# A transformer block in fp32: the MLP on four tiles at a time, attention items of eight heads, and the residual in DRAM

## The chip, the core and the metric

The kernel runs on one core of a Trainium2 chip. Its engines are TensorE (PE, with weight loads as PEld), VectorE (DVE), ScalarE (ACT), GpSimd (POOL) and SyncE (SP, which issues every DMA here). The metric is device time in microseconds; smaller is better. The kernel before takes 536.42 us, the median of 3 runs from 535.81 to 536.80.

## The reference

One sequence of S=2048 tokens with D=512. The block is pre-norm attention followed by a pre-norm MLP, each with a residual. Attention has 32 heads of 16; a token looks at itself and at seven earlier tokens, two apart (W=8, dilation 2). The MLP has F=1792 hidden columns and a squared ReLU.

```python
def _A_ref(x, wqkv, wo):
    qkv = (x @ wqkv).reshape(B, S, 3, H, Dh)   # q, k, v by head
    idx = pos[:, None] - off[None, :]          # off = arange(8) * 2
    logits = jnp.einsum("bhsd,bhswd->bhsw", q, kg) * scale
    logits = jnp.where(mask[None, None, :, :], logits, -1e9)
    attn = _softmax(logits, axis=-1)
    o = jnp.einsum("bhsw,bhswd->bhsd", attn, vg)
    return o.reshape(B, S, D) @ wo

def _B_ref(x, w1, b1, w2, b2):
    h = jnp.einsum("bsd,df->bsf", x, w1) + b1
    r = jnp.where(h > zero, h, zero)
    return jnp.einsum("bsf,fd->bsd", r * r, w2) + b2

h = x + _A_ref(_layernorm(x), A_wqkv, A_wo)
h2 = h + _B_ref(_layernorm(h), B_w1, B_b1, B_w2, B_b2)
```

## The kernel before

**Precision.** Every operand of a product is split into a high part, rounded to fp32r by ACT (`hi`, L115), and the rest, subtracted by DVE or POOL (`lo`, L118). A product is three sums of four matmuls over K: high by high, low by high, high by low (`mm3`, L172 to L177). Each matmul's shape in the profile is the number of columns that it streams.

**Tiles.** The 2048 tokens are 16 tiles of 128. The even and odd tokens of each half form a chain, so that the dilated window is contiguous rows of a chain; a chain of a half is four tiles. An index s from 0 to 7 stands for a pair of tiles (RI=2).

**The qkv stage.** For each tile and each of four column groups, 12 matmuls of 384 columns; ACT evacuates (`evac`, L412), and SP stores q, k and v into a DRAM scratch `qkv_d` (`store`). The first four tiles run group by group while the weights are prepared, then pairs of tiles (`first_phase`). Meanwhile `weight_job` loads and splits wo and w1.

**Attention.** An item is a pair s and a group pair of 8 heads, 32 items in all. Its windows of k and v come from `qkv_d`, as two halves j of four heads each, in two buffers a half. For s=0 and s=1 one load of 11 rows serves both. DVE multiplies q and k (`dots`, L272), sums over the head (L306, L320), adds the mask in the first half, subtracts the maximum (L333, L335); ACT exponentiates (L339); DVE sums, inverts and scales (L302, L309, L315) and multiplies with v (`weigh`, L283); POOL adds the eight window rows in a tree of three additions (L292), whose last one writes `o`. The halves j go one after the other. `attention()` is a generator: it yields the planned DVE time of what it has just written, and an item's second half is interleaved with the first half of the next item.

**Order.** The program is written slot by slot. `at` and `after` set chores for a slot; `end_slot` adds the slot's planned PE time, runs the chores, and lets `pump` take attention steps while the planned DVE time (times SLOW=1.1) is behind the planned PE time. `o_T(s, j)` first pumps until the items of s are written, then transposes o on PE; `wo_product` multiplies by wo into a `tr` bank; `h_add` (DVE, L475) adds the residual and takes statistics; `h_norm` (ACT, POOL) normalises and adds b2 to the residual, which stays in SBUF; `h_T` transposes the normalised tile.

**The MLP.** For each pair s, 14 hidden blocks f: `mlp1` is 12 matmuls of 256 columns (both tiles) into one of two `mm` banks; `hidden` is ReLU, square and cast on ACT (L509, L510, L115) and the low part on POOL, or on DVE for the last pair (HV=7); `mlp2` of block f-3 (LAG=3) is three matmuls of 512 columns for each tile into its accumulator bank, `acc0` or `acc1`. In the slots of pair s the o transposes of s+1 come at f=3 and 4 and its wo products at f=6 and 7. `finish` (DVE, L537) adds the residual, and SP writes the output. w2 is loaded and split during s=0 into the memory that wqkv had.

PSUM has eight banks: two `tr`, two `mm`, `acc0`, `acc1`, one for q (`qp`) and one for the exponentials (`ex`). SBUF rows of 2 KB are shared by many names under one tag with 15 buffers (ROWS).

## Time and profile before

| | us |
|---|---|
| median of 3 runs | 536.42 |
| the profiled execution, its own time | 534.84 |
| its span, first to last instruction | 533.1 |
| PE busy | 520.7 |
| PEld busy | 479.1 |
| DVE busy | 376.1 |
| POOL busy | 317.9 |
| ACT busy | 262.1 |

The granted clock was 1.00 over the whole span. A row of a group gives the line, engine, operation, tiles (out<-in), shapes and count; after the first bar the busy time and the mean duration in ns; after the second the idle time of that engine just before those instructions and what ended it. A row of a timeline begins with the start and the duration in us; a row with x4 is four in succession, and its duration is that of the four together, with the drain of the last. Matmuls overlap, so their cost is read from start to start. A row of windows gives the stretch, its length, the busy time and count of PE, PEld, DVE, ACT and POOL, the clock, the share of the DMA engines and GB/s. A row of DMA issues gives the count, the size of one and the median time from issue to landing.

### The profile page before, as it was taken

To read this page: it belongs to the slowest core of one execution; us is meant where nothing else is said; L and a number is where in the kernel's file an instruction comes from. 1 tells how busy PE (TensorE), PEld (TensorE's weight loads), DVE (VectorE), ACT (ScalarE), POOL (GpSimd) and SP (SyncE) were. 2 spreads that over 40 slices of the span, in tenths; PEclk is the share of its full clock that TensorE was granted. 3 is DMA by queue.
4 is the path that set the end of the run, shared out by engine and by line. 5 is a ranking of instruction groups with operands and counts; after the bars stand their busy time and mean duration, and the time that the engine had idled before them with its cause. 6 is when DMAs were issued, how large, how long until landed. Compare 5 with 4: busy or idle time off the path is not lost.

```text
span 533.1 us, 9022 instructions
## 1 busy us (share of the span) xinstructions
PE 520.7 (98%) x3186; PEld 479.1 (90%) x3186; DVE 376.1 (71%) x569; ACT 262.1 (49%) x607; POOL 317.9 (60%) x435
## 2 busy tenths in 40 slices
PE   6999999999999989999999999999999999999996
PEld 5899999999999868988989898898989889898995
DVE  5569999887897898996998699599869502202111
ACT  4524554455248446545636454563645445254541
POOL 4515499687495398778678677867867852251000
PEclk9999999999999999999999999999999999999999
DMA  8577979687587453633643364364434102001001
GB/s 251 155 233 196 298 234 317 201 269 239 159 252 263 135 157 91 191 116 102 182 142 108 111 190 119 100 183 137 112 106 140 44 0 81 1 0 41 2 0 41
DMA packets 70661, 75.96 MB, mean 143 GB/s; under 512 B 6744, under 2 KB 47704, under 8 KB 70616
## 3 DMA queue, kind: packets, MB, share of 16 engines
q1 hardware_dynamic: 70616, 75.39, 46.7%
q8 instruction: 25, 0.41, 0.3%
q14 instruction: 20, 0.16, 0.1%
HBM read 58.50 MB, written 16.91 MB: 141 GB/s over the span
## 4 chain that ended last, share of the span: by engine, by line
PE 61%; POOL 2%; DVE 0%; ACT 0%; issue 0%; POOLq 0%
PE mm L177 27%; PE acc L530 9%; PE acc L532 9%; PE acc L531 9%; PE wo L177 6%; PE tr L155 2%; POOL pr L292 1%; POOL rl L118 1%; POOL h L483 0%; POOL rs L134 0%; DVE pr L283 0%; POOL rs L132 0%; DVE h L537 0%; ACT hh L115 0%; POOL o L292 0%
## 5 line engine op out<-in xcount | busy, mean ns | idle before, releaser
L292 POOL TENSOR_TENSOR pr<-pr 128x512 f32<-128x512 f32 (+1 forms) x128 | 133.0, 1039 | 47.6 <-DVE pr L283 42.5
L118 POOL TENSOR_TENSOR rl<-r,rh 128x256 fp32r<-128x256 f32 x98 | 72.1, 739 | 82.9 <-ACT rh L115 73.6
L509 ACT ACTIVATE r<-mm,b_sb 128x256 f32<-128x256 f32 x112 | 53.3, 476 | 123.1 <-PE mm L177 112.3
L272 DVE TENSOR_TENSOR pr<-qp,k 128x1024 f32<-128x1024 f32 x64 | 76.0, 1187 | 5.8 <-ACT qp L216 3.5
L283 DVE TENSOR_TENSOR pr<-ex,v 128x1024 f32<-128x1024 f32 x64 | 77.9, 1217 | 2.8
L532 PE MATMUL acc<-w_h,rl 128*128 128x512 f32 x192 | 75.0, 391 | 2.7 <-POOL rl L118 2.7
L530 PE MATMUL acc<-w_h,rh 128*128 128x512 f32 x192 | 76.5, 398 | 0.0
L531 PE MATMUL acc<-w_l,rh 128*128 128x512 f32 x192 | 75.9, 395 | 0.0
L177 PE MATMUL mm<-hh,w_h 128*128 128x256 f32 x448 | 72.5, 284 | 0.0
L177 PEld LDWEIGHTS mm<-hh,w_h 128*128 128x128 f32 x448 | 66.4, 189 | 6.5
L177 PE MATMUL mm<-hl,w_h 128*128 128x256 f32 x448 | 72.0, 283 | 0.0
L177 PE MATMUL mm<-hh,w_l 128*128 128x256 f32 x448 | 72.0, 283 | 0.0
L177 PEld LDWEIGHTS mm<-hl,w_h 128*128 128x128 f32 x448 | 61.8, 192 | 0.0
L177 PEld LDWEIGHTS mm<-hh,w_l 128*128 128x128 f32 x448 | 61.7, 192 | 0.0
L412 ACT COPY y<-mm 128x384 f32<-128x384 f32 x64 | 30.1, 480 | 63.6 <-PE mm L177 40.0
L177 PE MATMUL mm<-wq_h,xh 128*128 128x384 f32 x256 | 56.7, 342 | 0.3 <-ACT wq_h L115 0.3
L177 PE MATMUL mm<-wq_l,xh 128*128 128x384 f32 x256 | 55.3, 335 | 0.2 <-DVE wq_l L118 0.2
L177 PE MATMUL mm<-wq_h,xl 128*128 128x384 f32 x256 | 55.0, 335 | 0.4 <-DVE xl L118 0.4
L118 DVE TENSOR_TENSOR hl<-tr,hh 128x256 fp32r<-128x256 f32 x32 | 12.1, 418 | 56.8 <-ACT hh L115 56.8
L510 ACT ACTIVATE r<-r 128x256 f32<-128x256 f32 x112 | 46.9, 418 | 3.5
L115 ACT CAST rh<-r 128x256 fp32r<-128x256 f32 x112 | 45.6, 407 | 3.6
L532 PEld LDWEIGHTS acc<-w_h,rl 128*128 128x128 f32 x192 | 36.1, 188 | 11.8 <-POOL rl L118 3.6
(78 smaller groups left out, 869.3 us busy)
## 6 DMA issues: line engine op xcount, KB each, us to landing
k<-qkv_d SPq DMA_DIRECT2D x48, 288.0 KB, 2.8
v<-qkv_d SPq DMA_DIRECT2D x48, 288.0 KB, 2.7
qkv_d<-y SPq DMA_DIRECT2D x32, 384.0 KB, 3.9
xt<-in_A_x_dram SPq DMA_DIRECT2D x16, 256.0 KB, 4.2
q<-qkv_d SPq DMA_DIRECT2D x32, 128.0 KB, 2.8
h<-in_A_x_dram SPq DMA_DIRECT2D x16, 256.0 KB, 4.0
out_dram<-h SPq DMA_DIRECT2D x16, 256.0 KB, 3.2
raw<-in_B_w_dram SPq DMA_DIRECT2D x16, 224.0 KB, 4.3
```

What stands on the lines that cost most here:

```text
L115: nc.scalar.copy(dst, src)
L118: eng.tensor_tensor(out=dst, in0=src, in1=h, op=ALU.subtract)
L177: nc.tensor.matmul(ps, l(k), r(k), start=(n == 0), stop=(n == 3 * KB - 1))
L272: nc.vector.tensor_tensor(out=pr.rearrange("p i w h d -> p i w (h d)"), in0=qp[:, j].unsqueeze(2).to_broadcast([P, RI, W, GC]), in1=kwin, ...
L283: nc.vector.tensor_tensor(out=p2, in1=vwin, op=ALU.mult, in0=e1[:, :, :, j * GH:(j + 1) * GH].unsqueeze(4).to_broadcast([P, RI, W, GH, DH]))
L292: nc.gpsimd.tensor_tensor(out=dst, in0=p2[:, :, :w], in1=p2[:, :, w:2 * w], op=ALU.add)
L412: nc.scalar.copy(y[:, :, t % RI * GC:(t % RI + 1) * GC], ps[:, :3 * GP].rearrange("p (j c) -> p j c", j=6))
L509: nc.scalar.activation(r, ps, AF.Relu, bias=b1_sb[:, f:f + 1])
L510: nc.scalar.activation(r, r, AF.Square)
L530: nc.tensor.matmul(a, rh[:, js], w2_h[f], start=(f == 0), stop=False)
L531: nc.tensor.matmul(a, rh[:, js], w2_l[f], start=False, stop=False)
L532: nc.tensor.matmul(a, rl[:, js], w2_h[f], start=False, stop=(f == FB - 1))
```

## The change

Three things change together, and the constants of the plan with them.

*Attention.* G becomes 4: a group has eight heads and 128 columns, and an item is done with one `dots`, one sum and one `weigh` of 2048 elements a partition. k and v have one buffer each of nine rows, loaded for every s, also for s=1. q, ex and the maximum share one PSUM bank (`att`).

*MLP.* The pairs are put in GROUPS of (2, 2, 2, 1, 1): three groups of four tiles and two of two. A wide group streams 512 columns in `mlp1`; its units are single products, first mlp1(f), then mlp2(f-2), alternately (LAG=2). It uses `acc0` to `acc3`, two `mm` banks and one `tr` bank. The transposed activations lie in `actT_h` and `actT_l`, one buffer that the qkv stage uses too. The hidden block's ReLU is written back to PSUM. While a wide group runs, the o transposes of the next group's tiles come at units 12, 15, 18 and 21 and their wo products two units later. `g < HV` (4) puts the low part on POOL for all but the last group.

*Residual.* `h_norm` stores h plus b2 into a DRAM scratch `h_d`; it is loaded again before `finish` (`load_out`): the first two tiles' near the end of the group, the last two of a wide group's after the accumulation, between the finishes. ROWS becomes 7.

```diff
-G = 8
+G = 4
-ROWS = 15
-LAG = 3
-SLOW = 1.1
+ROWS = 7
+LAG = 2
+SLOW = 1.05
-HV = 7
-WJ = 2
+GROUPS = (2, 2, 2, 1, 1)
+HV = 4
...
+    h_d = dram.tile([NS, RI, P, D], F32, name="h_d")
+    actT_h = wpool.tile([P, R, KB, P], F32R, name="actT_h")
+    actT_l = wpool.tile([P, R, KB, P], F32R, name="actT_l")
+    sq = wpool.tile([P, R * P], F32, name="sq")
...
+    att_ps = psum.tile([P, D], F32, name="att")
...
+        def dots(n):
+            pr = att.tile([P, RI, W, GH, DH], F32, name="pr")
+            nc.vector.tensor_tensor(
+                out=pr.rearrange("p i w h d -> p i w (h d)"),
+                in0=qp.unsqueeze(2).to_broadcast([P, RI, W, GC]),
+                in1=window(ks[n], [1, GC]), op=ALU.mult)
+            load_k(n + 1)
+            return pr
...
+        hn[s, j] = row("hn")
+        norm_apply((s, j), hn[s, j], h, nc.scalar)
         nc.gpsimd.tensor_tensor(out=h, in0=h, in1=b2_sb, op=ALU.add)
+        nc.sync.dma_start(h_d[s, j], h)
...
+        nc.scalar.activation(ps, ps, AF.Relu, bias=b1_sb[:, f:f + 1])
+        nc.scalar.activation(r, ps, AF.Square)
+        hi(rh, r)
...
+    def mlp1(g, n, f):
+        ps = psum.tile([P, n * P], F32, name="mm", tag="mm", bufs=2)
+        fs = slice(f * P, (f + 1) * P)
+        mm3(ps, lambda k: w1_h[:, k, fs], lambda k: w1_l[:, k, fs],
+            lambda k: actT_h[:, :n, k, :], lambda k: actT_l[:, :n, k, :])
+        at(1, hidden, g, n, f, ps)
+
+    def mlp2(f, acc, js):
+
+        rh, rl = hid[f]
+        for l, r, last in ((rh, w2_h, False), (rh, w2_l, False), (rl, w2_h, True)):
+            for j in js:
+                nc.tensor.matmul(acc[j], l[:, j * P:(j + 1) * P], r[f],
+                                 start=(f == 0 and l is rh and r is w2_h),
+                                 stop=(f == FB - 1 and last))
...
+    O_T, WO, H_T = (34, 36, 38, 40), (36, 38, 40, 42), (44, 45)
...
+    for n, t in enumerate(groups[0]):
+        if n >= 2:
+            h_T(t, n)
+    run(due)
...
+        if wide:
+            steps = [12 + 3 * n for n in range(len(nxt))]
...
+        for j, t in enumerate(tiles):
+            if j >= 2:
+                at(0, load_out, t)
+            at(0, finish, t, acc[j])
```

## The prediction

> **What bounds the kernel now.** First the page: busy shares, then the chain of work that ended last.

> ```profile
> span 533.1 us, 9022 instructions
> PE 520.7 (98%) x3186; PEld 479.1 (90%) x3186; DVE 376.1 (71%) x569; ACT 262.1 (49%) x607; POOL 317.9 (60%) x435
> PE 61%; POOL 2%; DVE 0%; ACT 0%; issue 0%; POOLq 0%
> ```

> PE is the bound, and what counts is its spacing from start to start, not its busy time. The chain in order of time merges twelve matmuls into a row:

> ```profile
> 407.03 1.43 PE mm L177 x12
> 409.85 2.72 PE wo L177 x12
> ```

> Twelve of 256 columns take 1.43 us, 119 ns each; twelve of 512 columns take 2.72, 227 ns each. PE's timeline gives the other forms, and PE's waits:

> ```profile
> 183.81 0.64 PE L177 MATMUL mm<-hh,w_h 128*128 128x256 f32 x4
> ...
> 185.25 0.40 PE L530 MATMUL acc<-w_h,rh 128*128 128x512 f32 x1
> ...
> 186.63 0.64 PE L177 MATMUL mm<-hh,w_h 128*128 128x256 f32 x4
> ...
> 192.27 0.50 PE L532 MATMUL acc<-w_h,rl 128*128 128x512 f32 x1 [0.75 <-POOL rl L118]
> ...
> 200.17 0.50 PE L532 MATMUL acc<-w_h,rl 128*128 128x512 f32 x1 [1.99 <-POOL rl L118]
> ...
> 126.55 0.85 PE L177 MATMUL mm<-wq_h,xl 128*128 128x384 f32 x4
> 127.24 0.86 PE L177 MATMUL mm<-wq_l,xh 128*128 128x384 f32 x4
> 127.94 0.60 PE L155 MATMUL tr<-ident,o 128*128 128x128 f32 x4
> 128.29 0.95 PE L177 MATMUL mm<-wq_h,xh 128*128 128x384 f32 x4
> ```

> The second product (L530 to L532) has six matmuls from 185.25 to 186.63, 230 ns each; a slot of both products has 2.82 (183.81 to 186.63); the 384-column ones take 0.69/4 = 173 ns, four transposes 0.35 us. So a matmul costs about 13 ns beyond 0.417 ns a column, whatever its width. After the start, PE waits only at the two marked rows, 2.7 us.

> Next I asked how late the attention is, since every o transpose on PE needs it. Windows, DVE's timeline and POOL's, and PE's:

> ```profile
> 46.70:240.00 193.30, 190.50 (x1150) 180.29 (x1149) 174.86 (x260) 99.48 (x226) 138.93 (x185) 1.00 0.68 208
> 45.45 1.21 DVE L283 TENSOR_TENSOR pr<-ex,v 128x1024 f32<-128x1024 f32 x1
> 236.49 1.23 DVE L283 TENSOR_TENSOR pr<-ex,v 128x1024 f32<-128x1024 f32 x1
> 237.63 1.21 DVE L320 TENSOR_REDUCE lg<-pr 128x64 f32<-128x1024 f32 x1
> 238.76 1.22 DVE L283 TENSOR_TENSOR pr<-ex,v 128x1024 f32<-128x1024 f32 x1
> 244.72 0.47 POOL L292 TENSOR_TENSOR o<-pr 128x128 f32<-128x128 f32 x1
> 260.33 0.60 PE L155 MATMUL tr<-ident,o 128*128 128x128 f32 x4
> ```

> The first item's last weighing ends at 46.7, the sixteenth's (last of s=3) at 240.0, its sum on POOL at 245.2, and PE fetches s=3 at 260.3: 15 us of margin. Fourth figure of the window: DVE is busy 174.9 of 193.3 us, idle 18.4.

> **The change, part by part.** *First product.* 1008 matmuls of 256 columns become 504 of 512: 2x119.2 - 226.7 = 11.7 ns each, **-5.9 us**. Bounds: -5.9, or 0 if a moving operand in four pieces of 128 (actT) costs the 13 ns back; the nearest row, wo, has whole rows; I take -5.9. [...] The rows above have 13 ns at all three widths, and the measurement decides.

> *Second product.* In the wide groups 504 of its matmuls run four tiles in a row on one w2 slice, at 230 ns before. Bounds 0 and -1.5 us (504 x 3 ns, down to wo's 227); I take **-0.7**.

> *The two POOL waits* go: mlp2(f) now stands four units (11 us) behind mlp1(f), where it stood three slots of 2.82 us. What is late next is not rl but o, below. **-2.7** (bounds -2.7 and 0).

> *Attention instructions.* Rows by line and shape:

> ```profile
> L283 DVE TENSOR_TENSOR pr<-ex,v 128x1024 f32<-128x1024 f32 x64 | 77.9, 1217 | 2.8
> L315 DVE TENSOR_TENSOR ex<-ex,sm 128x128 f32<-128x128 f32 x32 | 9.1, 283 | 0.0
> L335 DVE TENSOR_TENSOR lg<-lg,mx 128x128 f32<-128x128 f32 x32 | 19.3, 602 | 1.1
> L333 DVE TENSOR_REDUCE mx<-lg 128x16 f32<-128x128 f32 x32 | 12.5, 390 | 0.0
> L302 DVE TENSOR_REDUCE sm<-ex 128x16 f32<-128x128 f32 x32 | 8.9, 279 | 8.1 <-ACT ex L339 8.1
> L292 POOL TENSOR_TENSOR pr<-pr 128x512 f32<-128x512 f32 x64 | 84.7, 1323 | 42.6 <-DVE pr L283 42.5
> L292 POOL TENSOR_TENSOR pr<-pr 128x256 f32<-128x256 f32 x64 | 48.3, 755 | 5.0
> L118 POOL TENSOR_TENSOR rl<-r,rh 128x256 fp32r<-128x256 f32 x98 | 72.1, 739 | 82.9 <-ACT rh L115 73.6 <-issue 9.2
> ```

> L283 against L315 is 1.04 ns an element, so 2048 elements take 2.28 us where two of 1024 took 2.43 (2.2 from start to start, where one of 1024 has 1.14: 236.49, 237.63, 238.76). Three such pairs save 0.45 us an item, and mx in PSUM brings L335 nearer to L315, 0.32: some 0.8 us an item, 12 over fifteen items. A POOL chain of three adds takes 2.46 + 1.32 + 0.76 = 4.5 us. None of this is on PE's path by itself; it is worth what it brings o forward.

> *The deadline moves.* Group 0 holds four tiles, and s=3 is fetched within it. From the first o transposes (127.94, 53 of 64 qkv done, 14 of 16 tiles transposed) PE has eleven qkv of 12x173 ns = 22.9, six wo = 16.3, 18 units of 12x228 ns = 49.3 and twelve sets of transposes = 4.3 to do: 220.7, with the entry wait below **221.7**, against 260.3. DVE: 46.7 + 174.9 - 12 = 209.6 if it never idles, 228 if it idles as before; with POOL's 4.5 us o is ready between 214.1 and 232.5. Two orders tie it to PE's time T at that place. DVE's ol of (2,1) follows that tile's transposes at T-11.3, and after ACT's copy DVE does 0.6 + 2.2 + 0.75 + 2.2 us: weighing done at T-4.5. POOL does rl of f=9 first: that product ends one second product and one wo before T, at T-5.5, ACT's three operations take 1.9, rl 1.3, so the adds start at T-2.2 and o is ready at T+2.3 or later. Bounds +0 (PE never waits) and +10.8 (232.5); I take **+2.4**, by the tied rows. Where ACT's 1.9 is from: 256 columns have 1.30, and 512 some 0.21 more each (oh 584 against hh 375 ns):

> ```profile
> L509 ACT ACTIVATE r<-mm,b_sb 128x256 f32<-128x256 f32 x112 | 53.3, 476 | 123.1 <-PE mm L177 112.3 <-POOL rl L118 9.5
> L510 ACT ACTIVATE r<-r 128x256 f32<-128x256 f32 x112 | 46.9, 418 | 3.5
> L115 ACT CAST rh<-r 128x256 fp32r<-128x256 f32 x112 | 45.6, 407 | 3.6
> L115 ACT CAST hh<-tr 128x256 fp32r<-128x256 f32 x32 | 10.3, 375 | 22.0 <-PE tr L155 22.0
> L115 ACT CAST oh<-tr 128x512 fp32r<-128x512 f32 x16 | 9.3, 584 | 5.6 <-PE tr L155 4.1 <-DVE w_l L118 1.5
> ```

> *Group entry.* The last two h_T stand directly ahead of the first wide product, so PE waits for ACT's copies: 0.27 for a transpose to end and 2x0.58 us, less the second's transposes, 0.35: **+1.0** (0, if ACT lies ahead, to +2, if an evacuation stands before them).

> *The residual in DRAM.* At a wide boundary SP's order is out 0, out 1, load hf 2, out 2, load hf 3, out 3; each out waits for DVE, and DVE's finish of tile 2 and 3 for the load. Issues and landings:

> ```profile
> 211.07 0.89 SPq L539 DMA_DIRECT2D out_dram<-h  x2
> out_dram<-h SPq DMA_DIRECT2D x16, 256.0 KB, 3.2
> h<-in_A_x_dram SPq DMA_DIRECT2D x16, 256.0 KB, 4.0
> k<-qkv_d SPq DMA_DIRECT2D x48, 288.0 KB, 2.8
> L537 DVE TENSOR_TENSOR h<-acc,h 128x512 f32<-128x512 f32 x16 | 10.5, 683 | 4.3 <-PE acc L532 4.2
> ```

> Finishes 0 and 1 end about 1.4 us after the boundary; then twice (issues 0.6 + landing L + finish 0.68): with L of 2.8, 4.0 and 3.2 between them, tile 3 is finished at 9.6, 12.0 or 10.4. PE wants acc3 after three units and three matmuls, 8.9. Two boundaries matter (before the narrow groups acc2 and acc3 are not accumulators): 2 x 0.7 to 2 x 3.1; I take **+2.4**. Queued behind on SP: k of the next item but one; behind finish on DVE: the whole attention, 8 to 9 us. In group 1 h_add(4,0) must free the only tr bank for the next o transposes. DVE has fourteen long instructions of 2.2, four shares of 0.73 (L302, a reciprocal and L315, start to start), five shifts of 0.64 (L333 and L335 without its wait), ol and h_add ahead, 38 us, and ends at 10.4 + 38 = 48.4; PE is there after 15 units, one wo and one set of transposes, 44.1. With PE's own 1.2 lost that is 3.1 short if DVE's sum is exact; bounds 0 and 5; I take **+1.5**. In group 2 the next o is asked for later and the loss is hidden.

> *Hidden.* k and v single-buffered: a k load starts when dots ends and has logits, shares, weighing and shift (6 us) to land; 576 KB at 2.8 us for 288 lands in some 4 to 5. Reloading k and v for s=1 adds some 4 MB before 126 us, where DMA is at its fullest:

> ```profile
> 80.00:100.00 20.00, 20.00 (x122) 19.93 (x121) 18.33 (x28) 9.86 (x21) 17.28 (x23) 1.00 0.93 288
> ```

> There the cover is thin; what it costs is DVE idle, part of the 0 to 10.8 above. ACT's three wide operations (some 1.9 us) fit in 5.5; the h_d writes wait for POOL and share SP with k and v.

> *Sum.* -5.9 - 0.7 - 2.7 + 2.4 + 1.0 + 2.4 + 1.5 = **-2.0 us**, of which -9.3 is gain. The profiled execution took 534.84 us (span 533.1), so 532.8 there; the median of the runs shown is 536.42, 1.6 above it, so **534.4**.

> **The rivals.** *A. Attention falls behind (slower).* DVE idles in the first half as before (18.4 us), so o of s=3 comes at 232.5 and PE stands 10.8 us rather than 2.4; the same idle share (9.5%) over group 1's 38 us adds 3.6. 534.4 + 8.4 + 3.6 = **546.4**. It decides once DVE idles over 10 us between 47 and 217 (209.6 + 10 + 4.5 = T+2.4). For it: the deadline comes forward by 39 us while DVE gains 12, and DMA at 0.93. Against: part of the 18.4 was DVE waiting for PE, which costs nothing when DVE is late.

> *B. All waits hide (faster).* DVE is early at every finish and every o, and the hf loads land in under 2.8 us. Only gains: 536.4 - 9.3 = **527.1**; with the second product's bound 526.3 (another 0.8). For it: item idle in the early rows is small. Against: POOL's in-order place behind rl.

> *C. The wide product is not cheaper.* Four pieces per moving operand cost the 11.7 ns back: **540.3**. For it: no row shows that operand. Against: 13 ns is the same at 256, 384 and 512. [...]

> **How the numbers follow.** Forecast 0.42, A 0.27, B 0.24, C 0.07. The measurement tells 0.2% (1.1 us) from nothing. The forecast's own range, 531 to 538, is centred 2.0 below before: 0.28 faster, 0.08 the same, 0.06 slower. B adds 0.24 to faster; A and C 0.34, of which 0.02 falls in the middle (A in part) and 0.32 is slower. Faster 0.52, same 0.10, slower 0.38. The range reaches from just under B's lower end, 526, into A, 546.

> **What would show it.** Wide mm rows at twelve to 2.72 us (C wrong); finish rows of the wide boundaries with DVE idle behind hf's DMA twice, and a PE gap before acc of tile 3 near 1 us; a PE gap at the o transposes of s=3 of 1 to 5 us (A: about 11, B: none); no PE wait for rl. Wrong altogether if PE stands in the qkv stage, where I count nothing, or if k's landing stops DVE on every item.

## The result, and the profile after

The changed kernel takes **590.56 us**, the median of 4 runs (588.18 to 591.21), where the kernel before, on the same chip, takes 536.12. The ratio is 1.1009, 95% interval 1.0973 to 1.1045: 54 us slower. The prediction, 534.4 with a range of 526 to 546, was wrong. The page of the profiled execution (its own time 588.18), cut to span, busy shares, PE's clock by slices, and the chain that ended last:

```profile
span 586.4 us, 7471 instructions
PE 533.6 (91%) x2682; PEld 463.5 (79%) x2682; DVE 379.0 (65%) x457; ACT 230.1 (39%) x465; POOL 291.5 (50%) x297
PEclk9999999999899997979999989988897999999999
PE 39%; DVE 31%; DMA 10%; POOL 9%; issue 4%; ACT 3%; SPq 2%; DVEq 0%; POOLq 0%; ACTq 0%
```

Before, PE had 61% of the chain and no other engine over 2%; now DVE, DMA and POOL have half of it. The account can be made from these rows and those of before. PE stood 586.4 - 533.6 = 52.8 us, before 533.1 - 520.7 = 12.4: **40.4 us of new stalls**. PE's busy time rose by 12.9 us, and 40.4 + 12.9 = 53.3 is the difference of the spans. The busy time rose although the work became cheaper: with the clock at 1.00 throughout, the same 2682 PE instructions take 516.2 us (pool_light, below), 4.5 less than before. So some 17 us have to be explained, and most of them are stretches in which the clock was granted at half: the trace has seven, 41 us in all, in which PE was busy 29.6 us, twice what that work needs at full clock (twelve matmuls 5.27 us against 2.72, below). That is **some 15 us**; the other 2 to 3 are not accounted for. Where PE stood, from the windows up to the first wide product and on from there:

```profile
46.00:178.90 132.90, 123.93 (x705) 118.21 (x704) 111.39 (x138) 55.12 (x120) 86.10 (x96) 0.99 0.73 243
180.00:586.40 406.40, 367.72 (x1752) 305.67 (x1752) 236.90 (x277) 153.63 (x302) 190.19 (x170) 0.95 0.34 111
```

and from its waits (us in total, times, longest):

```profile
PE wo L187 <- DVE ol L123: 14.3, 4, 5.3
PE tr L171 <- DVE actT_l L123: 10.2, 3, 6.4
PE tr L171 <- POOL o L302: 5.3, 1, 5.3
PE acc L539 <- DVE hf L550: 4.1, 2, 3.4
```

Nine microseconds in the qkv stage (132.90 - 123.93), where before it never stood, and 39 behind it, where before it stood some 7; the longest waits are for DVE. PE's timeline shows both what was right and what a stall costs:

```profile
207.06 1.07 PE L539 MATMUL acc<-w_h,rh 128*128 128x512 f32 x4
...
209.78 1.07 PE L187 MATMUL mm<-actT_h,w_h 128*128 128x512 f32 x4
...
212.50 1.07 PE L539 MATMUL acc<-w_h,rh 128*128 128x512 f32 x4
...
226.66 2.07 PE L187 MATMUL wo<-wo_h,oh 128*128 128x512 f32 x4 [5.34 <-DVE ol L123]
...
231.93 1.08 PE L187 MATMUL mm<-actT_h,w_h 128*128 128x512 f32 x4
```

Twelve wide matmuls take 2.72 us (209.78 to 212.50), as predicted. The twelve of wo behind a stall of 5.34 take 5.27 (226.66 to 231.93). The windows (the clock is the third figure from the end) say why:

```profile
218.00:225.00 7.00, 3.31 (x15) 2.42 (x13) 6.93 (x6) 3.40 (x7) 5.72 (x4) 1.00 0.26 85
225.10:231.90 6.80, 5.24 (x12) 4.13 (x13) 6.64 (x9) 0.66 (x2) 1.18 (x1) 0.50 0.45 148
231.90:246.00 14.10, 14.10 (x65) 11.47 (x63) 13.73 (x17) 5.61 (x10) 8.07 (x8) 1.00 0.43 134
```

The stall begins at 221.3; some 3.7 us into it the clock goes to 0.50, and it stays there for 6.8 us. Another 6.8 us of half clock begin in each of the stalls near 247, 332, 389 and 444 us, and 3.4 us in the one at 147 us and behind the one at 417 us.

**POOL's chain.** Groups of POOL's adds and of DVE's mask add, the same add (L325) before, and POOL and DVE on the timeline of after:

```profile
L302 POOL TENSOR_TENSOR pr<-pr 128x1024 f32<-128x1024 f32 x32 | 77.7, 2428 | 79.4 <-DVE pr L295 79.4
L302 POOL TENSOR_TENSOR pr<-pr 128x512 f32<-128x512 f32 x32 | 41.2, 1288 | 2.5
L302 POOL TENSOR_TENSOR o<-pr 128x256 f32<-128x256 f32 x32 | 24.2, 756 | 2.5
...
L270 DVE TENSOR_TENSOR lg<-lg,mask 128x128 f32<-128x128 f32 x16 | 15.9, 996 | 0.0
```

```profile
L325 DVE TENSOR_TENSOR lg<-lg,mask 128x128 f32<-128x128 f32 x16 | 6.6, 412 | 0.2
```

```profile
206.20 4.13 POOL L302 TENSOR_TENSOR pr<-pr 128x1024 f32<-128x1024 f32 x2 [4.37 <-DVE pr L295]
206.64 2.48 DVE L270 TENSOR_TENSOR lg<-lg,mask 128x128 f32<-128x128 f32 x1
```

An item's adds are now one stretch of 2.43 + 1.29 + 0.76 = 4.5 us, and what the program has behind it on POOL came after it in the trace; before, a half's three adds were 2.5. DVE's mask add, of the same size as before, takes 2.48 us in these rows, as long as POOL's first add beside it (2.43 on average). What else stands behind the adds on POOL: the weight splits of the qkv stage. SP's and ACT's waits between 46 and 180 us, of after and of before:

```profile
SPq L460 <- POOL w_l L123: 20.4, 4, 5.4
SPq L460 <- POOL rs L137: 7.3, 2, 5.8
ACT y L419 <- DMA qkv_d<-y: 49.5, 16, 6.5
```

```profile
SPq L450 <- POOL w_l L118: 3.5, 1, 3.5
ACT y L412 <- DMA qkv_d<-y: 10.4, 5, 3.6
```

The weight loads (L460) took rows of a ring of 15 before; now they share the five buffers of rl and rh, which POOL frees late. (The smaller number of buffers is not the reason by itself: pool_only below has the same five, and SP's 20.4 us are 5.8 there.) SP's queue stands behind them, the stores stand behind SP, and ACT waits for a free y. The three small POOL operations that give the second norm its factors (`rs`) stand behind the adds too. ACT's waits for them over the whole span, of after and of before:

```profile
ACT hn L155 <- POOL rs L141: 45.9, 10, 8.0
```

```profile
ACT hn L150 <- POOL rs L136: 6.8, 3, 3.9
```

Lastly the boundary at 290 us, SP, DVE and PE:

```profile
290.52 0.32 SPq L211 DMA_DIRECT2D v<-qkv_d  x1
291.12 0.94 SPq L552 DMA_DIRECT2D out_dram<-hf  x2
292.15 0.44 SPq L545 DMA_DIRECT2D hf<-h_d  x1
298.00 0.33 SPq L552 DMA_DIRECT2D out_dram<-hf  x1
298.43 0.37 SPq L545 DMA_DIRECT2D hf<-h_d  x1
...
297.28 0.69 DVE L550 TENSOR_TENSOR hf<-acc,hf 128x512 f32<-128x512 f32 x1 [5.58 <-DMA hf<-h_d]
301.24 0.69 DVE L550 TENSOR_TENSOR hf<-acc,hf 128x512 f32<-128x512 f32 x1 [3.27 <-DMA hf<-h_d]
...
301.98 0.50 PE L539 MATMUL acc<-w_h,rh 128*128 128x512 f32 x1 [3.42 <-DVE hf L550]
```

The order is the predicted one, load, finish, out, load, finish; the first load, issued behind a load of v, lands 5.0 us after its issue, and DVE waits 8.9 us in two pieces with one finish between them.

### The profile page after: what moved, and what is told of

It is laid out like the page before. It is cut to its first block, busy times and chain, and to the rows that moved or that the text cites. A ratio compares the mean times of both kernels' runs of the same rounds, so it can differ in the third digit from the quotient of the medians.

```text
span 586.4 us, 7471 instructions
## 1 busy us (share of the span) xinstructions
PE 533.6 (91%) x2682; PEld 463.5 (79%) x2682; DVE 379.0 (65%) x457; ACT 230.1 (39%) x465; POOL 291.5 (50%) x297
## 4 chain that ended last, share of the span: by engine, by line
PE 39%; DVE 31%; DMA 10%; POOL 9%; issue 4%; ACT 3%; SPq 2%; DVEq 0%; POOLq 0%; ACTq 0%
PE mm L187 16%; PE acc L539 15%; DVE pr L295 8%; PE wo L187 7%; DVE pr L254 6%; DVE lg L263 5%; POOL pr L302 5%; DMA xt<-in_A_x_dram 4%; DMA hf<-h_d 2%; DVE lg L270 2%; PE tr L171 2%; DMA h<-in_A_x_dram 1%; DVE actT_l L123 1%; DVE w_l L123 1%; DVE st L131 1%
## 5 line engine op out<-in xcount | busy, mean ns | idle before, releaser
L302 POOL TENSOR_TENSOR pr<-pr 128x1024 f32<-128x1024 f32 x64 | 118.9, 1858 | 81.9 <-DVE pr L295 79.4
L123 POOL TENSOR_TENSOR rl<-sq,rh 128x512 fp32r<-128x512 f32 (+1 forms) x56 | 64.4, 1151 | 115.4 <-ACT rh L120 61.6
L295 DVE TENSOR_TENSOR pr<-att,v 128x2048 f32<-128x2048 f32 x32 | 73.3, 2291 | 4.6 <-DMA v<-qkv_d 1.9
L254 DVE TENSOR_TENSOR pr<-att,k 128x2048 f32<-128x2048 f32 x32 | 73.0, 2280 | 4.7 <-ACT att L248 3.6
L263 DVE TENSOR_REDUCE lg<-pr 128x128 f32<-128x2048 f32 x32 | 73.0, 2280 | 0.6
L187 PE MATMUL mm<-actT_h,w_h 128*128 128x512 f32 (+1 forms) x280 | 65.6, 357 | 1.2 <-ACT actT_h L120 1.2
L187 PE MATMUL mm<-actT_l,w_h 128*128 128x512 f32 (+1 forms) x280 | 63.1, 347 | 1.9 <-DVE actT_l L123 1.9
L187 PE MATMUL mm<-actT_h,w_l 128*128 128x512 f32 (+1 forms) x280 | 64.1, 351 | 0.0
L187 PE MATMUL mm<-wq_h,actT_h 128*128 128x384 f32 x256 | 58.2, 349 | 1.6 <-ACT actT_h L120 1.1
L539 PE MATMUL acc<-w_h,rh 128*128 128x512 f32 x192 | 54.9, 396 | 4.1 <-DVE hf L550 4.1
L187 PE MATMUL mm<-wq_h,actT_l 128*128 128x384 f32 x256 | 55.6, 338 | 0.8 <-DVE actT_l L123 0.7
L539 PE MATMUL acc<-w_h,rl 128*128 128x512 f32 x192 | 54.1, 394 | 2.2 <-POOL rl L123 2.2
L123 DVE TENSOR_TENSOR actT_l<-tr,actT_h 128x512 fp32r<-128x512 f32 x32 | 21.6, 684 | 50.6 <-ACT actT_h L120 50.5
L539 PE MATMUL acc<-w_l,rh 128*128 128x512 f32 x192 | 53.6, 390 | 0.0
L518 ACT ACTIVATE sq<-mm 128x512 f32<-128x512 f32 (+1 forms) x70 | 35.9, 513 | 32.6 <-POOL rl L123 28.4
## 6 DMA issues: line engine op xcount, KB each, us to landing
xt<-in_A_x_dram SPq DMA_DIRECT2D x16, 256.0 KB, 6.5
h<-in_A_x_dram SPq DMA_DIRECT2D x16, 256.0 KB, 4.3
h_d<-h SPq DMA_DIRECT2D x16, 256.0 KB, 2.0
hf<-h_d SPq DMA_DIRECT2D x16, 256.0 KB, 2.9
```

The lines of the kernel that those rows point to most:

```text
L123: eng.tensor_tensor(out=dst, in0=src, in1=h, op=ALU.subtract)
L187: nc.tensor.matmul(ps, l(k), r(k), start=(n == 0), stop=(n == 3 * KB - 1))
L254: nc.vector.tensor_tensor(out=pr.rearrange("p i w h d -> p i w (h d)"), in0=qp.unsqueeze(2).to_broadcast([P, RI, W, GC]), in1=window(ks[n] ...
L263: nc.vector.tensor_reduce(out=lgs[n], in_=pr, axis=X, op=ALU.add)
L295: nc.vector.tensor_tensor(out=p2, in1=window(vs[n], [DH, GH], [1, DH]), op=ALU.mult, in0=ex.unsqueeze(4).to_broadcast([P, RI, W, GH, DH]))
L302: nc.gpsimd.tensor_tensor(out=dst, in0=p2[:, :, :w], in1=p2[:, :, w:2 * w], op=ALU.add)
```

## The experiments

Each is the changed kernel but for the edits named. PE idle is span less PE's busy time, clock the mean granted clock, both of the profiled execution (before: 12.4 and 1.00). Several medians lie within 3 us of their neighbours; such steps count only together with the trace.

| run | median (range) us | to before, 95% | PE idle | clock |
|---|---|---|---|---|
| the change | 590.56 (588.18 to 591.21) | 1.1009 [1.0973, 1.1045] | 52.8 | 0.965 |
| hf_early | 570.47 (565.35 to 573.43) | 1.0637 [1.0573, 1.0702] | 39.2 | 0.981 |
| mask_psum | 585.69 (582.29 to 588.87) | 1.0930 [1.0882, 1.0979] | 48.7 | 0.962 |
| store_act | 586.77 (583.55 to 589.32) | 1.0948 [1.0895, 1.1002] | 50.7 | 0.956 |
| three_mends | 560.51 (560.00 to 562.05) | 1.0458 [1.0438, 1.0479] | 33.6 | 0.978 |
| clock_fill | 585.91 (585.38 to 588.65) | 1.0946 [1.0916, 1.0976] | 41.1 | 0.974 |
| two_tile | 600.40 (598.91 to 603.91) | 1.1216 [1.1175, 1.1257] | 54.6 | 0.974 |
| rl_behind | 573.74 (572.35 to 575.08) | 1.0708 [1.0683, 1.0734] | 43.7 | 0.973 |
| rs_ahead | 570.02 (566.90 to 571.85) | 1.0620 [1.0585, 1.0655] | 39.1 | 0.973 |
| rs_only | 555.66 (551.34 to 558.49) | 1.0352 [1.0299, 1.0406] | 30.0 | 0.978 |
| rl_three | 577.23 (575.53 to 579.59) | 1.0765 [1.0732, 1.0797] | 45.6 | 0.966 |
| dve_light | 552.00 (550.75 to 552.39) | 1.0288 [1.0264, 1.0312] | 29.1 | 0.984 |
| pool_light | 536.55 (532.94 to 538.30) | 0.9993 [0.9972, 1.0015] | 18.6 | 1.00 |
| pool_only | 554.12 (553.80 to 556.88) | 1.0358 [1.0331, 1.0385] | 30.7 | 0.985 |
| split_alone | 570.74 (570.12 to 572.09) | 1.0660 [1.0640, 1.0680] | 40.4 | 0.979 |
| split_mended | 546.81 (545.39 to 549.17) | 1.0219 [1.0185, 1.0253] | 22.4 | 0.989 |
| rl_on_dve | 544.37 (541.28 to 545.68) | 1.0156 [1.0120, 1.0192] | 20.5 | 0.991 |
| rl_later | 541.50 (539.28 to 542.90) | 1.0098 [1.0061, 1.0134] | 21.9 | 0.997 |
| own_bank | 538.62 (534.70 to 540.78) | 1.0047 [1.0010, 1.0084] | 18.2 | 0.994 |

### The residual back early: hf_early

```diff
-            if n in (S - 4, S - 3):
+            if 0 <= n - S + 4 < len(tiles):
                 at(0, load_out, tiles[n - S + 4])
...
-            if j >= 2:
-                at(0, load_out, t)
             at(0, finish, t, acc[j])
```

> The changed kernel with all four residual tiles of a wide group loaded back in its last four units, ahead of the boundary, instead of two ahead and two between the finishes. Theory H (the finishes stop DVE at the wide boundaries, and the attention behind them is late for the next group): DVE's 22.1 us of waits for these loads fall under 4, PE's stall of 3.4 at the first boundary goes, those at the first wo of groups 1 and 2 (4.4 and 4.1) and the 2.8 of the second boundary shrink with their stretches of half clock, and the time comes to 568 to 580. Rival A (the attention itself is too slow for the new deadlines): DVE's waits for the loads go, the stalls of group 1 and 2 stay over two thirds, the time comes to 584 to 591.

20 us won, the largest single mend. DVE's four finishes of the first boundary now run in a row:

```profile
287.19 2.48 DVE L550 TENSOR_TENSOR hf<-acc,hf 128x512 f32<-128x512 f32 x4
```

The stall of 3.42 is gone, and so is the stall at the first wo of group 1, which begins 40 us later; that of group 2 falls from 4.1 to 2.5. Theory H holds: at the two boundaries themselves PE had stood only 4.1 us (3.42 and 0.64). The rest is what DVE, stopped for 8.9 us at the first boundary and 6.5 at the second, was late for afterwards, and the clock: three stretches at half clock are left of seven, in which PE is busy 13.5 us instead of 29.6, worth some 8 of the 20.

### The mask in PSUM: mask_psum

```diff
+    mask_ps = att_ps[:, NM:NM + R * W].rearrange("p (r w) -> p r w", r=R)
...
-                    in1=mask[:, i0:i0 + RI].unsqueeze(3).to_broadcast([P, RI, W, GH]))
+                    in1=mask_ps[:, i0:i0 + RI].unsqueeze(3).to_broadcast([P, RI, W, GH]))
...
+    nc.scalar.copy(mask_ps, mask)
```

> The changed kernel with the mask copied once to PSUM, in free columns of the attention's bank, so that the mask add (L270) has one operand in SBUF and one in PSUM instead of two in SBUF. Theory L (the add with two SBUF operands stands still while POOL's 1024-element add runs): its mean falls from 996 ns to about 300, DVE has 11 us less to do in the first half, the two stalls of 5.3 us in group 0 get shorter by 3 to 8 us together, the time comes to 580 to 587. Rival (the add is long for another reason, or its length does not matter): the mean stays near 1 us, or falls while the time stays at 589 to 592.

Rows of DVE by form, the add and the weight split:

```profile
L272 DVE TENSOR_TENSOR lg<-lg,att 128x128 f32<-128x128 f32 x16 | 4.3, 270 | 0.0
L123 DVE TENSOR_TENSOR w_l<-raw,w_h 128x512 fp32r<-128x512 f32 x12 | 13.1, 1093 | 1.7 <-ACT w_h L120 1.7
```

The add falls from 996 to 270 ns, as theory L has it. A third of that comes back: w_l, which also has two SBUF operands, goes from 803 to 1093 ns; that it now meets POOL's add in the mask add's place is argued, not shown. The rows go with the length of POOL's first add: 412 ns beside adds of 1.3 us (before), 996 beside 2.4 (the change). Why the mask add lasts longer there, no run shows. In pool_only below, where POOL's first two adds are gone and the mask is in SBUF, the mask add takes 440 ns. The stall at the first wo of group 0 falls from 5.34 to 1.42 us, but a wait of 2.00 for DVE's residual add comes 8 us behind it, and the time gained, 5 us, is at the edge of what the intervals tell apart.

### The stores from ACT's queue: store_act

```diff
-        nc.sync.dma_start(chain(e, g, 0, PAD + CH // 2 * b + i,
+        nc.scalar.dma_start(chain(e, g, 0, PAD + CH // 2 * b + i,
```

> The changed kernel with one thing different: the stores of q, k and v (L405) are issued from ACT's queue, right behind the copy that fills them, no longer from SP's. Theory Q (SP's queue): in the qkv stage SP's queue stands 30 us in all behind weight loads whose buffers POOL frees late, the stores stand in line behind them, so ACT's copy waits 49.5 us for a free y buffer and PE 11.4 us for a bank between 46 and 179 us. Then ACT's wait for the stores falls under 15 us, PE's stalls in that stage under 5 us, and the time comes to 574 to 584. Rival D (DVE is the limit, the store is late because everything is): ACT's wait stays over 35 us, PE's stalls over 8, and the time 586 to 592.

ACT's waits, 46 to 180 us:

```profile
ACT y L419 <- PE mm L187: 19.9, 15, 3.2
ACT y L419 <- DMA qkv_d<-y: 13.2, 8, 3.1
```

The wait for the stores fell as expected, and the time did not (the interval overlaps that of the change). PE still stood 7 of its 9 us there, now longest for DVE's actT_l copies. The blocked stores were real but not last: theory Q falls as a cause by itself.

### Together: three_mends

> The three edits at once: stores from ACT's queue, mask in PSUM, residual loaded back early. If the three causes are separate, the gains add up: about 9 + 6 + 15 us, 556 to 566, and the granted clock is back to 0.98 or more because it is lost only behind stalls. If one lateness lies behind all stalls, the gain is about that of the best single edit, 570 to 580. A result under 536 would say that the four-tile product itself is worth having.

30 us, as much as the three together (20 + 5 + 4): this is what separate causes would give, though the 5 and the 4 are each at the edge of the noise. 25 us over the kernel before remain.

### The clock: clock_fill

```diff
+        if (s, j) in ((2, 0), (4, 0), (6, 0)):
+            fill = psum.tile([P, D], F32, name="fill", tag="mm", bufs=2)
+            for n in range(18):
+                nc.tensor.matmul(fill, w1_h[:, 0, :P], wo_h[:, n % KB, :], start=True, stop=True)
```

> The changed kernel with 18 idle matmuls of 512 columns (4.1 us, into a free bank, their result unused) put on PE ahead of the first output projection of the three four-tile groups that prepare another tile, where PE stood 5.5, 4.5 and 4.2 us for DVE. Theory G (after a stall of some 4 us the clock is granted at half for 6.8 us, whatever ended the stall): the three stretches of half clock at 225, 334 and 447 us go, the next matmuls run at full spacing, and about 3 x 2.7 us are won although PE does more: 580 to 585. Rival (the half clock has another cause, or costs nothing because PE waits again behind it): the stretches stay, or they go and the time stays at 589 to 593.

PE's timeline at the first of the three places, and its window:

```profile
224.95 4.24 PE L500 MATMUL fill<-wo_h,w_h 128*128 128x512 f32 x18
229.51 1.20 PE L187 MATMUL wo<-wo_h,oh 128*128 128x512 f32 x4 [0.32 <-DVE ol L123]
```

```profile
225.00:231.90 6.90, 6.58 (x29) 5.13 (x28) 6.83 (x8) 0.66 (x2) 4.01 (x4) 1.00 0.37 115
```

With the fill the clock stays at 1.00 at all three places, and from the o transposes to the end of that wo PE takes 13.5, 12.9 and 13.0 us instead of 16.9, 15.7 and 15.6: 8.8 us won there with more work. The median moved by 4.7 only, and the two intervals just overlap; the clock was lost elsewhere: stalls of 1.99 and 3.58 us at 184 and 302 us brought half clock here, and their like in the change (1.95 and 3.42) had not. Theory G holds at the place, and its sum is not shown. In the change each of the five stalls of over 4 us (4.09 to 6.38) brought 6.8 us of half clock; of the shorter ones, those of 3.48 and 2.21 brought 3.4, and those of 3.42 and 1.95 none.

### Two-tile groups: two_tile

```diff
-GROUPS = (2, 2, 2, 1, 1)
+GROUPS = (1,) * 8
-HV = 4
+HV = 7
...
-    O_T, WO, H_T = (34, 36, 38, 40), (36, 38, 40, 42), (44, 45)
+    O_T, WO, H_T = (34, 36), (36, 38), (44, 45)
...
+                while (items[old][0] - 2, 1) not in fetched and items[old][0] >= 2:
+                    yield None
```

> The changed kernel with two tiles in every group of the MLP, so 256 columns in the first product and no four-tile group; the eight-head attention, the stores and the residual in DRAM stay as they are (the attention is kept from running more than two tile pairs ahead, since o has two buffers). Theory W (the four-tile groups ask for attention earlier than DVE and POOL can give it): after 180 us PE's stalls fall from 38 us to under 6, the 11 to 14 us lost in the qkv stage stay, time 546 to 558. Rival A (the eight-head items are too slow themselves, whatever the groups): over 20 us of stalls stay after 180, time 565 to 585.

Slower still. PE's waits:

```profile
PE acc L543 <- POOL rl L123: 36.9, 15, 6.2
```

A two-tile slot is 2.8 us and LAG is 2, so rl has 5.6 us to come, and it stands on POOL behind 4.5 us of adds. PE no longer waits for o or ol, as theory W has it for the later deadlines, but the chain now meets rl instead: the 11 us between the products of a four-tile group hide it, two-tile groups with LAG=2 do not. How much of this is LAG=2 and rl's two buffers, and how much the eight-head items, no run parts. The time went against both theories, and pointed to POOL.

### POOL's order: rl_behind, rs_ahead, rs_only, rl_three

```diff
-            at(0, lo, nc.gpsimd, rl, r, rh)
+            after(0, lo, nc.gpsimd, rl, r, rh)
```
```diff
-        if delay:
+        if delay and type(key) is not tuple:
             after(0, finish)
```
```diff
-        rl = work.tile([P, n * P], F32R, name="rl", bufs=2)
+        rl = work.tile([P, n * P], F32R, name="rl", bufs=3)
```

rl_behind has the first edit on three_mends, rs_ahead the first two, rs_only the second alone, rl_three the third (with one buffer for q and one for lg).

> The three mends, and POOL's rl (L123) put behind the attention's adds of its slot instead of ahead of them. Theory P (tied orders: the adds of the last item of s=3 stand on POOL behind an rl that waits 3.3 us for a buffer that PE frees, and PE waits for the adds): the stall of 5.75 us at the third o transpose of group 0 falls under 2.5 and its half clock goes, 560.5 becomes 551 to 557. Rival (POOL's order is not what is late, or rl now comes late for PE): a PE wait for rl of the same size appears, 559 to 566.

> As the run before, and the three small POOL operations of the second norm (L137 to L141) directly behind its statistics, ahead of the adds of that slot. Theory P: the stall of 6.2 us at the last hn transpose of the second boundary (hn waits 7.4 us for rs, which stands behind 4.5 us of adds) falls under 2.5; with both 543 to 551. Rival: DVE's statistics are late themselves, the stall moves from rs to DVE and the time stays within 3 us of the run before.

> The three mends, and the three small POOL operations of the second norm directly behind its statistics, ahead of the adds of that slot, with rl where it was. Theory P: the stall of 6.2 us before the last hn transpose of the second boundary falls under 2 with its half clock, 552 to 556. Rival: POOL now waits in order for late statistics, the adds and rl behind it come later, 559 to 570.

> The three mends, and rl has three buffers instead of two (q and lg one each to make room), so that POOL's rl need not wait for PE before the adds that stand behind it. Theory P': the 3.3 us that POOL waited ahead of the adds of s=3 go, the stall of 5.75 us becomes 1.5 to 3 and keeps full clock: 555 to 558. Rival: rl was not what held the adds (DVE's weighing ended at the same time), or the single q and lg buffers cost DVE what rl gains: 559 to 566.

On three_mends only rs_only gained: 4.9 us, the stall of 6.05 before the last hn transpose gone, ACT's waits for rs down from 47.0 to 11.9 us. The same move on rl_behind, rs_ahead, gave 3.7. Putting every rl behind the adds cost 13 us: ACT's square waits for rl in the single sq buffer, 55.9 us in all instead of 13.2, and PE's stalls at the first wo of groups 1 and 2 grew from 0 and 2.4 to 4.6 and 4.5 us. rl_three says nothing on rl: DVE waited 42 us for the single lg buffer, which it had not done before.

### Who is late, DVE or POOL: dve_light, pool_light

```diff
-            nc.vector.tensor_reduce(out=lgs[n], in_=pr, axis=X, op=ALU.add)
+            nc.vector.tensor_reduce(out=lgs[n], in_=pr[:, :, :, :, :2], axis=X, op=ALU.add)
```
```diff
-            w = W // 2
+            w = 1
             while w:
```

> The three mends, and the sums of the logits take 2 of the 16 products of a head (14 of 16 are left out: the reduce has 256 elements instead of 2048, some 0.35 us instead of 2.28, about 1.9 us of DVE less per item, 30 us over the first sixteen items). Theory D: DVE's throughput sets when o comes, so the stalls of the first wo and of o of s=3 go, and the qkv stage loses under 4 us: 540 to 549. Rival P: POOL's order behind rl keeps the 5.75 us and the 6.2 us where they are, 551 to 559. In both the item's other waits (k, v, exponent) show how much of DVE's gain is used.

> The three mends, and of POOL's three adds of an item only the last is left (the first two are left out, so POOL's chain is 0.75 us instead of 4.5; o is then not the whole sum). Theory P (the remaining stalls in the MLP come from POOL's long chain in its fixed order): the 5.75 us at o of s=3 and the 6.2 us before the last hn transpose fall under 1.5 each with their half clock, 560.5 becomes 543 to 550. Rival D (DVE is late itself): the stall at the first wo of group 0 and those of the qkv stage stay and the others move to DVE's work, 553 to 560.

Taking 1.87 us an item off DVE (2280 to 414 ns), 30 us in the first half, won 8.5 us, of it some 3 in the qkv stage, where PE's stalls fell from 3.8 to 0.5; the stalls of 5.58 at o of s=3 and 6.07 before hn stayed (5.57 and 6.05 in three_mends). Taking 3.7 us an item off POOL won 24, more than the expected 10 to 17, and brought the time to that of the kernel before (both edits leave out the work that their expectations name). The page of pool_light:

```profile
PE 516.2 (97%) x2682; PEld 453.9 (85%) x2682; DVE 368.2 (69%) x457; ACT 234.3 (44%) x466; POOL 174.1 (33%) x233
PE 66%; DVE 20%; DMA 5%; issue 4%; ACT 2%; POOL 2%; SPq 1%; DVEq 0%; POOLq 0%; ACTq 0%
```

DVE's 368.2 us are within 3 of the 370.9 of three_mends, and yet PE has 66% of the chain, where it had 53%, and the clock is 1.00 throughout. What was late in three_mends was mostly POOL.

### Alone, and by length: pool_only, split_alone, split_mended, rl_on_dve

```diff
+            def adds(i):
+                w = W // 2
+                while w:
+                    dst = p2[:, i, :w] if w > 1 else o_t[s][:, i, g * GC:(g + 1) * GC].rearrange(
+                        "p (w h d) -> p w h d", w=1, h=GH)
+                    nc.gpsimd.tensor_tensor(out=dst, in0=p2[:, i, :w], in1=p2[:, i, w:2 * w],
+                                            op=ALU.add)
+                    w //= 2
+            adds(0)
             load_v(n + 1)
+
+            def rest():
+                adds(1)
+                done[s] += 1
+            return rest
...
             if new:
                 shift(n)
                 yield 1.0
+            if old is not None:
+                rest()
```

pool_only has the w = 1 of pool_light on the change itself, split_alone the split alone, split_mended the split on rs_only, and rl_on_dve also HV=2.

> The changed kernel, not mended, with the first two of POOL's three adds of an item left out (o is then not the whole sum). Theory P (POOL's chain lies behind most of the stalls, those at the finishes too): 590.6 becomes 536 to 550. Theory S (the causes stand beside each other: the late residual costs about 20 us whatever POOL does): 24 us less than 590.6, 562 to 570, with DVE's waits for the residual still near 20 us.

> The changed kernel with POOL's adds of an item in two halves, one for each of o's two tiles (512, 256 and 128 elements each), the second half one step later, so that other work can stand between them; all work is kept, and POOL's busy time grows by about 0.7 us an item. Theory G (the length of the uninterrupted stretch costs): the stall at o of s=3 and those behind rs shrink, 575 to 585. Rival W (POOL's total work costs): 590 to 600.

> The same split of the adds, on the three mends with rs directly behind its statistics (555.7). Theory G: the 5.7 us at o of s=3 go to under 3, 545 to 552. Rival W: 555 to 562.

> As split_mended, and rl of the groups from the third on comes from DVE (0.68 us for 512 elements in the same form of operation) instead of POOL (1.29). If POOL's queue is what is late in the third group: 2 to 6 us under split_mended. If DVE is (its ol ends last at the first wo there): the stall of 5.3 us at that wo grows and the time is 0 to 5 us over split_mended.

pool_only lies between its two theories: 36 us won, where pool_light won 24 on the mends, and DVE still waits 19.7 us for the residual. So the chain and the mended causes stand beside each other, with an overlap of some 12 us. PE's stalls in the qkv stage, 9 us in the change, are 2.7 in pool_only and 4.0 in split_alone. split_alone decides the question of length: all work is kept, POOL's busy time rises from 291.5 to 309.6 us, and 20 us are won. Its rows by form:

```profile
L304 POOL TENSOR_TENSOR pr<-pr 128x512 f32<-128x512 f32 x64 | 83.6, 1307 | 66.6 <-DVE pr L295 66.6
...
L270 DVE TENSOR_TENSOR lg<-lg,mask 128x128 f32<-128x128 f32 x16 | 8.6, 535 | 0.0
```

With the longest POOL operation at 1.3 us the mask add is back to 535 ns. The split does three things: it shortens the stretch, has o's first tile ready before the second, and with its shorter operations takes 7 us off DVE's mask adds (15.9 to 8.6); the runs do not part them. split_mended, without that third effect (its mask is in PSUM), still won 8.9 us over rs_only, inside the range that theory G gave, though of the 5.48 us at o of s=3 a total of 3.47 stay: 1.65 for POOL's o and 1.82 for DVE's residual add. rl_on_dve's 2.4 us are in the expected direction, but the two intervals touch.

### The tied order, and the best version: rl_later, own_bank

rl_later is rl_on_dve with the first edit, own_bank has both.

```diff
-            at(0, lo, nc.gpsimd, rl, r, rh)
+            at(1 if (g, f) == (0, 9) else 0, lo, nc.gpsimd, rl, r, rh)
```
```diff
-        banks(*(("tr",) if wide else ("tr", "acc2", "acc3")))
+        banks(*(("mm", "tr") if wide else ("tr", "acc2", "acc3")))
```

> As rl_on_dve, with one instruction moved: POOL's rl of f=9 in the first group one unit later, behind the adds of the last item of s=3 rather than ahead of them. Theory (tied orders): the two stalls of 2.2 and 1.6 us at o of s=3 go and one stretch of half clock with them, 539 to 543. Rival (DVE's weighing ends so late that the order does not matter): 543 to 546.

> As the run before, and in the four-tile groups the output projection takes a bank of the first product's pair, so that transposes need not wait for the residual add and the projection not for ol's read. Theory: the 2.1 us at the second o transpose of group 0 (a wait for DVE's residual add) and half of the 1.3 and 1.9 us at the first wo of the next groups go, 535 to 540. Rival (the first product now waits for its bank, since DVE's add is late): 541 to 548. Under 534.5 would beat the kernel before.

rl_later: 2.9 us, with overlapping intervals, and one of the two stalls at o of s=3 (1.40, for POOL's o) gone. The other, 2.08, stayed: PE waits there for the bank that DVE's residual add frees, and that add stands behind a `dots` of 2.28 us. own_bank takes this wait away, and PE stands 2.90 us for POOL's o at the same place; its interval overlaps that of rl_later. It is the best version with four-tile groups here: 52 us better than the change, and still not faster than the kernel before (1.0010 to 1.0084). Its PE idles 18.2 us, 6 more than before, at the same busy time.

## Why the prediction was wrong

*The widths: right; the bound not.* The wide product costs 227 ns a matmul, and rival C is refuted. But PE's spacing, which had 61% of the chain before, no longer sets the time: PE has 39% of it. The second product, from 207.06 to the 209.78 above, takes 2.72 too, 227 each and 3 ns under before, the lower bound. Of the two rl waits one came back, 2.2 us at 417 us, so the -2.7 was -0.5.

*"None of this is on PE's path by itself": the step that failed.* The 4.5 us of POOL's chain were computed, and followed to one place only, o of s=3. The trace of before shows POOL in order with splits, rs and rl behind the adds, and its longest stretch was 2.5 us. Making it 4.5 delayed things that the sum had at nothing: the weight splits, and through SP's queue the stores; rs, and so hn at the second boundary (a stall of 6.4 us); rl (ACT's square waited 28.4 us for it, PE 2.2); and the mask add, and with it DVE. The qkv stage lost 9 us where "nothing" was counted, which the prediction had named as a sign of being wrong altogether; 2.7 are left with the short chain of pool_only. Which of the delays PE paid for there is open: with the stores off SP's queue (store_act) 7 of the 9 stayed. pool_light and pool_only put the whole chain at 24 and 36 us, split_alone the split of its stretch at 20.

*Attention instructions: half right.* The maximum in PSUM brought L335's 602 ns to 287, as said. But the mask add, which only the first sixteen items have, rose from 412 to 996: fifteen times 0.58 is 8.8 of the 12 us promised.

*o at s=3: right mechanism, size off.* The adds did stand behind an rl that waits for PE. POOL and PE:

```profile
246.31 1.27 POOL L123 TENSOR_TENSOR rl<-sq,rh 128x512 fp32r<-128x512 f32 x1 [3.31 <-PE acc L539]
247.54 3.69 POOL L302 TENSOR_TENSOR pr<-pr 128x1024 f32<-128x1024 f32 x2
251.30 0.72 POOL L302 TENSOR_TENSOR o<-pr 128x256 f32<-128x256 f32 x1
...
252.08 0.48 PE L171 MATMUL tr<-ident,o 128*128 128x128 f32 x1 [5.34 <-POOL o L302]
```

5.3 instead of 2.4: DVE's weighing had ended at 244.8, but rl waited for the buffer that the running second product held, not only for its turn, so the adds began at T+1.3 (T is 246.2 here) and not T-2.2. The stall at the first wo of group 0, also 5.3, was not in the sum at all: DVE was late for ol, in part through two mask adds of some 2.5 us (mask_psum).

*The residual: right order, mis-sized.* Predicted 2 x 1.2 at PE and 1.5 in group 1, 3.9 in all; hf_early shows 20. At the boundaries PE stood 3.42 and 0.64. The first load landed in 5.0 us, over the 4.0 bound, behind v on SP's queue, and DVE lost 22 us at three boundaries. The +1.5 for group 1 (bounds 0 to 5) was 4.4, and that in group 2 "the loss is hidden" was wrong: 4.1 there, of which 1.6 went with hf_early. The single buffers of k and v, which were feared, cost little: DVE stood 1.1 us for k and 1.9 for v.

*The clock: left out.* Every stall was priced at its length. In the trace seven stalls, 31 us in all, brought some 15 us of slow running on top, half again.

*Entry:* 3.1 us (1.16 and 1.95) for +1.0.

*Rival A* had the direction, and its condition held: DVE idled 23 us between 47 and 217 (busy 146.9 of 170) where 10 decided. Its sign did not come: the gap at o of s=3 was 5.3 us, near the forecast's 1 to 5 and not A's 11. Its price, 12 us, had the same holes: one place, no clock, no boundary.

## What to carry to other kernels

Merging instructions lengthened the stretch on POOL that nothing behind it got past, here from 2.5 to 4.5 us, and splitting it alone won 20 us (split_alone): for each merged chain list everything queued behind it on its engine, and who waits for that, down to DMA queues; its busy time says nothing of this (in split_alone POOL's rose from 291.5 to 309.6 us). Where a kernel has PE at 98%, a stall can cost more than its length: the seven here that were followed by half clock (2.2 to 6.4 us) cost half again as much. Reload what an epilogue needs before the boundary, not between its steps (hf_early: 20 us): the cost showed a group later.

## What was not expected of the hardware

```profile
302.00:312.00 10.00, 10.00 (x44) 8.29 (x45) 9.70 (x11) 4.25 (x8) 2.94 (x2) 1.00 0.37 114
...
419.70:422.90 3.20, 3.20 (x9) 2.46 (x8) 1.76 (x4) 2.90 (x7) 1.28 (x1) 0.50 0.01 4
```

The longer one cost nothing more, the shorter one 3.4 us at half clock. The two stalls of 5.34 that began at 221 and 247 us were each followed by 6.8.
